# Attention in plain float32 with two heads side by side in the array, issued as one group per unit, and a router that works in quarters of the array

## The chip, the cores and the metric

The kernel runs on one core of a Trainium2 chip. The metric is the device time of one execution in microseconds (us), with the kernel's inputs and its output in device memory. TensorE (PE) does the matmuls, VectorE (DVE), ScalarE (ACT) and GpSimd (POOL) the elementwise work, and SyncE (SP) issues most of the transfers.

## The reference

Attention over a window of 128 keys with a linear bias for each head, then a dense layer with a gate, then a mixture of eight experts of which each token uses one:

```python
q, k, v: (4, 8, 576, 64) float32
scores = q @ k.T / 8 + slope[head] * -(i - j)        # kept where 0 <= i - j < 128
attn   = softmax(scores)
x      = (attn @ v) as (2304, 512)
h      = x @ w_in                                    # (512, 2048)
x      = (h * clip(h + 3, 0, 6) / 6) @ w_out         # (2048, 512)
logits = (x / |x|) @ (expert_emb / |expert_emb|).T / tau
e      = argmax(logits);  gate = softmax(logits)[e]
out    = gate * (relu(x @ w1[e]) @ w2[e])
```

## The kernel before

The 2304 tokens are cut into nine chunks of 256. A **unit** is one chunk and one pair of heads, so each chunk has four. Units of chunks 0 and 1 (class `Early`) run at the start, while the dense layer's weights arrive. The other 28 (class `Unit`) run in pieces between the dense layer's matmuls of the chunk before: `gemm1` (L780, 24 matmuls of 256 columns) and `gemm2` (L823, 12 matmuls of 512 columns), eight of each in a chunk. After a chunk's `gemm2`, `Route` turns the rows of the result (L851), works out the eight logits of a token (L869) and ranks the tokens by expert (L897, L898). From about 600 us on only the experts' matmuls are left.

The dense layer and the experts use float32 split in two float32r parts, high and low, with three matmuls for a product. A `Unit` does the same: `split_qk` splits keys and scaled queries (L579 to L592) and copies the query parts across the partitions with two DMAs of ACT's queue, `split_v` splits the values, `split_p` the flipped probabilities. So a head's scores (L625) are two matmuls of 128 rows for each block of queries, and its values (L742) two for each window of keys. `Early` does it in plain float32: its scores (L420) use 64 rows of the array for a head, its values (L474) 64 columns, with the two heads next to each other. Flips (L461, L697) are transposes of the probabilities on PE.

A batch has 576 tokens, which is two and a quarter chunks. Chunks 3, 5 and 8 lie evenly on blocks of 128 rows. Chunks 2 and 6 have blocks of 64 rows of queries and of keys, chunk 7 has one block of 64 keys, and chunk 4 has blocks of 128 but a batch's start inside. 

PE's order is that of the program: a table `todo` maps a step (a number, some 3 us) to functions, and the steps are written out by hand (`UNITS_2`, `UNIT`, `PARTS`, `FIRST`, `ROUTE`). On DVE, ACT and POOL the program's scheduler sets the order in this part. Before, a unit has two pieces of scores, two of flips and two of values, one of each for a head, spread over the steps. `I_NORM`, `I_VHI`, `I_VLO`, `I_XLO`, `I_XL3` and `I_GL` are tables that choose the engine of some steps by chunk.

Of the kernel before, what the change touches and what calls it, by code (L numbers as in the profile page):

```python
# [46 lines left out]
SECOND_1 = 2.95  # L47

FIRST = (16.97, 1.91, 2.95)

UNITS_2 = (0.3, 2.8, 5.3, 7.8)
UNIT = (11.36, 3.6)


PARTS = (
    (2.28, 5.87, 8.0, 0.86, 1.01, 5.33, 5.0, 1.94),
    (3.01, 6.0, 8.3, 0.91, 1.0, 4.93, 4.79, 1.0),
)

ROUTE = ((3.76, 4.57, 6, 8.04), (1, 1.43, 2.92, 4.5))  # L60

I_NORM = (1, 1, 0, 1, 0, 0, 0, 0, 0)
I_VHI = (0, 1, 1, 0, 0, 0, 1, 1, 0)
I_VLO = (1, 1, 0, 0, 0, 0, 0, 0, 0)
I_XLO = (0, 1, 1, 0, 1, 1, 0, 0, 1)
I_XL3 = (1, 1, 1, 1, 1, 1, 1, 1, 1)
I_GL = (1, 0, 0, 0, 1, 0, 0, 0, 1)
# [18 lines left out]
def words(t):  # L86
    return t.bitcast(F32)
# [7 lines left out]
def tile_kernel(  # L95
# [41 lines left out]
    raw = right.enter_context(tc.tile_pool(name="raw", bufs=1, side="right"))  # L137
    at1 = right.enter_context(tc.tile_pool(name="at1", bufs=1, side="right"))
# [22 lines left out]

    def either(flag):
        return V if flag else nc.gpsimd
# [43 lines left out]
    enT = const.tile([128, KD, NE], F32, name="enT")  # L207
# [7 lines left out]
    nc.gpsimd.memset(half, 0.5)  # L215
    for p in range(NP):
        for h in range(2):
            nc.gpsimd.memset(units_of[64 * h:64 * h + 64, p:p + 1], unit_of(2 * p + h))
# [28 lines left out]
    def embed():  # L247
# [12 lines left out]
        V.tensor_copy(out=enT, in_=ps[:, :, 0:NE])  # L260
# [234 lines left out]
    class Unit:  # L495
# [55 lines left out]
        def load_v(self):  # L551
            t = raw.tile([128, len(self.ks), 128], F32, tag="vr", name="vr")
# [7 lines left out]
        def transpose_qk(self):  # L560
            def turn(src, width, nm):
                t = at1.tile([128, width], F32, tag=nm, name=nm)
                V.transpose(out=t, in_=src.rearrange("p t i -> p (t i)")[:, 0:width])
                return t
# [4 lines left out]
        def split_qk(self):  # L569


            nk = self.koff[-1]
            kT, qT = self.kT, self.qT
            self.k1 = k1 = at1.tile([128, 2, 384], F32R, tag="k1", name="k1")
            self.q1 = q1 = at1.tile([128, 2, CH], F32R, tag="q1", name="q1")
            self.q2 = q2 = at1.tile([128, 2, CH], F32R, tag="q2", name="q2")
            for h in range(2):
                r, o = slice(64 * h, 64 * h + 64), slice(64 - 64 * h, 128 - 64 * h)
                nc.scalar.copy(k1[r, h, 0:nk], kT[r, 0:nk])  # L579
                V.tensor_tensor(  # L580
                    out=k1[o, h, 0:nk], in0=kT[r, 0:nk], in1=words(k1[r, h, 0:nk]), op=ALU.subtract
                )
            for h in range(2):
                r, o = slice(64 * h, 64 * h + 64), slice(64 - 64 * h, 128 - 64 * h)
                sc = unit_of(self.h0 + h)
                nc.scalar.activation(out=q1[r, h, :], in_=qT[r, 0:CH], func=AF.Copy, scale=sc)
                V.scalar_tensor_tensor(
                    out=q1[o, h, :], in0=qT[r, 0:CH], scalar=sc, in1=words(q1[r, h, :]),
                    op0=ALU.mult, op1=ALU.subtract,
                )  # L590
# [3 lines left out]
        def split_v(self):  # L594

            self.v2 = v2 = at1.tile([128, 4, 2, 128], F32R, tag="v2", name="v2")
            spans = [(r, r + x[2]) for r, x in zip(self.row, self.ks)]
            for r0, r1 in sorted(set(spans)):
# [920 lines left out]
```

## Time and profile before

| what | value |
|---|---|
| time, median of 3 runs | 852.37 us (845.07 to 852.41) |
| the profiled execution | 850.65 us, of which its span is 848.9 us |
| mean granted clock of TensorE in the span | 0.968 of full speed |
| busy share of PE, DVE, ACT, POOL | 95%, 65%, 54%, 37% |

A row of a group of instructions gives line, engine, operation, tiles, shape and count. The timeline's first two columns are a start and a duration in us. Matmuls are pipelined, so a duration covers more than the array's own time for it. The distance from the start of one piece to the start of the next says what a piece costs in a dense stretch.

### The profile page before, as it was taken

To read this page: it belongs to the slowest core of one execution; us is meant where nothing else is said; L and a number is where in the kernel's file an instruction comes from. 1 tells how busy PE (TensorE), PEld (TensorE's weight loads), DVE (VectorE), ACT (ScalarE), POOL (GpSimd) and SP (SyncE) were. 2 spreads that over 40 slices of the span, in tenths; PEclk is the share of its full clock that TensorE was granted. 3 is DMA by queue.
4 is the path that set the end of the run, shared out by engine and by line. 5 is a ranking of instruction groups with operands and counts; after the bars stand their busy time and mean duration, and the time that the engine had idled before them with its cause. 6 is when DMAs were issued, how large, how long until landed. Compare 5 with 4: busy or idle time off the path is not lost. (4 is left out here: it accounts for less than half of the span.)

```text
span 848.9 us, 16092 instructions
## 1 busy us (share of the span) xinstructions
PE 809.2 (95%) x5404; PEld 721.3 (85%) x5404; DVE 551.0 (65%) x1482; ACT 459.2 (54%) x1140; POOL 314.5 (37%) x617
## 2 busy tenths in 40 slices
PE   5899989899999999999999999999999999999994
PEld 3666578679989999988899999998899999999993
DVE  4999967575767776867677776324565566447620
ACT  6676657466646566567467565333655445435410
POOL 1000014473544556776557645123233122132300
PEclk8699999899999999999999999999999999999997
DMA  9927133323333233233233221005647655465200
GB/s 263 332 81 221 79 69 67 44 58 80 58 56 83 47 65 81 52 58 72 43 58 86 50 48 29 2 25 165 221 133 239 226 182 197 169 217 177 100 24 26
DMA packets 156664, 90.86 MB, mean 107 GB/s; under 512 B 117491, under 2 KB 134003, under 8 KB 156576
## 3 DMA queue, kind: packets, MB, share of 16 engines
q1 hardware_dynamic: 148352, 72.85, 31.4%
q10 hardware_dynamic: 4480, 7.34, 4.0%
q0 software_dynamic: 3744, 9.58, 3.3%
q8 instruction: 45, 0.74, 0.4%
q14 instruction: 43, 0.35, 0.2%
HBM read 72.76 MB, written 9.74 MB: 97 GB/s over the span
## 5 line engine op out<-in xcount | busy, mean ns | idle before, releaser
L780 PE MATMUL h_ps<-xs,w_i 128*128 128x256 f32 x1536 | 202.3, 289 | 2.0 <-ACT xs L159 2.0
L780 PEld LDWEIGHTS h_ps<-xs,w_i 128*128 128x128 f32 x1536 | 192.1, 194 | 4.5 <-ACT xs L159 2.2
L823 PE MATMUL y_ps<-w_o,gh 128*128 128x512 f32 x512 | 167.0, 408 | 1.0 <-ACT gh L159 1.0
L823 PEld LDWEIGHTS y_ps<-w_o,gh 128*128 128x128 f32 x512 | 93.9, 193 | 18.8 <-ACT gh L159 1.3
L160 DVE TENSOR_TENSOR w_e<-st,w_e 128x1024 fp32r<-128x1024 f32 x64 | 77.4, 1233 | 47.8 <-ACT w_e L159 47.8
L1060 PE MATMUL ps_u<-x,w_e 128*128 128x280 f32 (+5 forms) x768 | 104.8, 293 | 0.0
L823 PE MATMUL y_ps<-w_o,gl 128*128 128x512 f32 x256 | 102.3, 400 | 1.4 <-POOL gl L160 1.4
L1060 PEld LDWEIGHTS ps_u<-x,w_e 128*128 128x128 f32 x768 | 100.0, 188 | 0.2
L797 DVE SCALAR_TENSOR_TENSOR u<-u,h_ps 128x512 f32<-128x512 f32 x72 | 49.2, 683 | 55.0 <-ACT u L790 54.7
L790 ACT ACTIVATE u<-h_ps,three 128x512 f32<-128x512 f32 x72 | 49.3, 684 | 65.4 <-PE h_ps L780 52.0
L659 ACT ACTIVATE pt<-pt,nm 128x128 f32<-128x128 f32 (+1 forms) x128 | 49.9, 391 | 61.9 <-DVE pt L648 24.8
L1084 PE MATMUL ps_o<-hs,w_e 128*128 128x280 f32 (+4 forms) x576 | 78.4, 295 | 0.0
L1084 PEld LDWEIGHTS ps_o<-hs,w_e 128*128 128x128 f32 x576 | 76.5, 188 | 0.0
L159 ACT CAST w_e<-st 128x1024 fp32r<-128x1024 f32 x64 | 65.3, 1049 | 15.4 <-DMA st<-in_moe_w_dram 6.0
L1159 POOL DMA_INDIRECT out_dram<-ob,ids x23 | 30.4, 1321 | 108.7 <-DVE ob L1158 99.4
L611 POOL TENSOR_TENSOR v<-vr,v 128x384 fp32r<-128x384 f32 (+4 forms) x48 | 35.6, 751 | 82.0 <-ACT v L608 79.8
L823 PEld LDWEIGHTS y_ps<-w_o,gl 128*128 128x128 f32 x256 | 49.1, 192 | 14.0 <-POOL gl L160 2.3
L159 ACT CAST gh<-u 128x512 fp32r<-128x512 f32 x64 | 39.6, 619 | 29.4 <-DVE u L797 28.8
L690 POOL TENSOR_TENSOR pt<-pt,rs 128x128 f32<-128x128 f32 (+2 forms) x80 | 33.6, 440 | 45.2 <-DVE rs L677 29.8
L1068 ACT ACTIVATE hs<-ps_u 128x280 fp32r<-128x280 f32 (+5 forms) x64 | 25.7, 404 | 45.3 <-PE ps_u L1060 44.0
L639 DVE CUSTOM_DVE_ANT_0 pt<-sc_ps,table 128x256 f32<-128x256 f32 (+3 forms) x128 | 44.1, 370 | 6.6 <-PE ps_pt L697 2.6
L1018 POOL DMA_INDIRECT xg<-ybuf,ids x20 | 22.9, 1145 | 55.8 <-DMA ids<-slots 41.9
(187 smaller groups left out, 1507.2 us busy)
## 6 DMA issues: line engine op xcount, KB each, us to landing
st<-in_moe_w_dram SPq DMA_DIRECT2D x32, 512.0 KB, 4.6
st<-in_moe_w_dram SPq DMA_DIRECT2D x16, 1024.0 KB, 8.9
wst<-in_moe_w_in_dram SPq DMA_DIRECT2D x8, 1024.0 KB, 8.6
wst<-in_moe_w_out_dram SPq DMA_DIRECT2D x8, 1024.0 KB, 8.6
q<-q ACTq DMA_DIRECT2D x56, 128.0 KB, 2.2
vr<-in_v_dram SPq DMA_DIRECT2D x72, 64.0 KB, 2.2
ybuf<-ys SPq DMA_DIRECT2D x18, 256.0 KB, 2.3
kr<-in_k_dram SPq DMA_DIRECT2D x48, 48.0 KB, 2.1
```

Source lines behind the costliest of these rows:

```text
L159: nc.scalar.copy(hi, src)
L160: eng.tensor_tensor(out=lo, in0=src, in1=words(hi), op=ALU.subtract)
L611: either(I_VLO[self.c]).tensor_tensor(out=d[:, :, 1::2, :], in0=s, in1=words(d[:, :, 0::2, :]), op=ALU.subtract)
L639: V.tensor_tensor_reduce(out=pt[0:n, s0:s1], in0=self.sc_ps[0:n, s0:s1], in1=table[0:n, t0:t0 + c1 - c0], scale=-slope, scalar=3.0e38, op0 ...
L659: nc.scalar.activation(out=pt[0:n, a:a + m], in_=pt[0:n, a:a + m], func=AF.Exp, scale=-1.0, bias=nm[0:n, j:j + 1], accum_out=sm[0:n, j:j + 1],
L690: nc.gpsimd.tensor_tensor(out=w, in0=w, in1=rs[0:n, j:j + 1].to_broadcast([n, m]), op=ALU.mult)
L780: nc.tensor.matmul(hp[:, f, :], lhsT=w[:, a, kk, f * 128:(f + 1) * 128], rhs=xs[:, b, kk, :], start=(n == 0), stop=(n == 3 * KD - 1),)
L790: nc.scalar.activation(out=u, in_=hp, func=AF.Relu, bias=three, scale=1.0)
L797: V.scalar_tensor_tensor(out=u, in0=u, scalar=6.0, in1=h_t[c, i], op0=ALU.min, op1=ALU.mult)
L823: nc.tensor.matmul(y_t[c][t], lhsT=g[a][:, f, t * 128:(t + 1) * 128], rhs=w[:, b, f, :], start=(i == 0 and f == 0 and n == 0), stop=(i == ...
L1060: nc.tensor.matmul(ps, lhsT=w[:, a, kk, (f % 2) * 128:(f % 2) * 128 + 128], rhs=x[:, b, kk, c0:c1], start=(n == 0), stop=(n == 3 * KD - 1),)
L1084: nc.tensor.matmul(ps, lhsT=ws_t[j, 4 + f // 2][:, a, f % 2, d * 128:(d + 1) * 128], rhs=hs[:, b, f, 0:width(j)], start=(n == 0), stop=(n ...
```

## The change

`Unit` is written like `Early`. The splits of queries, keys, probabilities and values, with their tiles and the two DMAs of the queries, go. Scores and values are plain float32 matmuls, with the two heads of a pair in two halves of the array. Normalising moves from ACT or POOL to DVE, the low parts of `x` and of the gated hidden values go to DVE throughout, and the tables that chose engines go. A unit's scores, flips and values no longer have steps of their own for each head: at each step of `group`, PE does the values of one unit, the flips of the next and the scores of the one after it, in a row. The loads get more buffers (`raw` two, `vr` three).

The logits are turned round. The embedding (32 columns, 8 of them used) is the stationary operand, four blocks of 128 model dimensions go into four quarters of the array's columns, ACT copies the result, and a second pair of matmuls (`total`) with a table of ones (`fold`) adds up the four quarters, one step of `TOTAL` later.

```diff
-PARTS = (
-    (2.28, 5.87, 8.0, 0.86, 1.01, 5.33, 5.0, 1.94),
...
+GROUPS = (1.9, 2.8, 15.7)
+PARTS = (1.2, 1.2, 6.0, 2.78)
+TOTAL = 0.95
...
-            nc.scalar.dma_start(out=words(q2)[0:64], in_=words(q1)[64:128])
-            nc.scalar.dma_start(out=words(q2)[64:128], in_=words(q1)[0:64])
...
+        def scale(self):
+            nc.scalar.activation(out=self.qT, in_=self.qT, func=AF.Copy, scale=units_of[:, self.p:self.p + 1])
...
-        def scores(self, h):
-            sc_ps = bank([128, 512], "sc_ps")
-            r = slice(64 * h, 64 * h + 64)
+        def scores(self):
+            self.sc = [bank([128, 512], "sc_ps") for h in range(2)]
             for j, n, c0, cm, c1, s0, s1 in self.blocks():
-                for a, qq in enumerate((self.q1, self.q2)):
+                for h in range(2):
+                    r = slice(64 * h, 64 * h + 64)
                     nc.tensor.matmul(
-                        sc_ps[0:n, s0:s1], lhsT=qq[:, h, self.qoff[j]:self.qoff[j] + n], rhs=self.k1[:, h, c0:c1],
-                        start=(a == 0), stop=(a == 1),
-                    )
+                        self.sc[h][0:n, s0:s1], lhsT=self.qT[r, self.qoff[j]:self.qoff[j] + n], rhs=self.kT[r, c0:c1],
+                        start=True, stop=True,
+                    )
...
-        def values(self, h):
+        def values(self):
             acc = bank([128, CH], "acc")
...
+                for h in range(2):
                     nc.tensor.matmul(
...
+                        acc[64 * h:64 * h + 64, o:o + m], lhsT=self.vr[k0:k0 + kn, kj, 64 * h:64 * h + 64],
+                        rhs=self.pp[h][k0:k0 + kn, at:at + m],
...
+            keep_x(self.c, self.p, acc, V)
...
-        split(gh, gl, g_t[c, i], either(not I_GL[c]))
+        split(gh, gl, g_t[c, i])
...
         def logits(self):
-            self.lg = lg = bank([128, 2, NE], "lg")
+
+            ps = bank([128, CH], "lgT")
             for t in range(2):
                 for kk in range(KD):
                     nc.tensor.matmul(
-                        lg[:, t, :], lhsT=self.yT[t][:, kk, :], rhs=enT[:, kk, :], start=(kk == 0), stop=(kk == KD - 1)
-                    )
+                        ps[32 * kk:32 * kk + 32, t * 128:(t + 1) * 128], lhsT=enT[:, kk, :], rhs=self.yT[t][:, kk, :],
+                        start=True, stop=True, skip_group_check=True,
+                    )
+            self.lgT = small("lgT", (128, CH), bufs=1)
+            nc.scalar.copy(self.lgT, ps)
+
+        def total(self):
+            self.lg = lg = bank([128, 2, NE], "lg")
+            for t in range(2):
+                nc.tensor.matmul(lg[:, t, :], lhsT=self.lgT[:, t * 128:(t + 1) * 128], rhs=fold, start=True, stop=True)
...
+    def group(n):
+        n -= n_early
+        return GROUPS[0] + GROUPS[1] * n if n < 5 else GROUPS[2] + 2 * FIRST[1] * (n - 5)
...
+        t0, t1, t2 = (group(n + x) for x in range(3))
+        turn, norm, early, vearly = PARTS
...
+        at(t0 - turn, u.scale)
+        at(t0, u.scores)
         for h in range(2):
-            d = b + h * other
...
+            at(t0, u.soften, h)
...
+        at(t1, u.flip_p)
+        for h in range(2):
+            at(t1, u.unload_p, h)
+        at(t2, u.values)
```

The first place is PE in the dense layer of chunk 4, where units of chunk 5 are done. Before, a head's flips (`ps_pt`) and another's scores (`sc_ps`, four matmuls with the two query parts in turn) stand between a `gemm2` and a `gemm1` (`h_ps`), and the values (`acc`, high and low probabilities `ph` and `pl` in turn) after it:

```order
L823 MATMUL y_ps<-w_o,gl 128x512
L697 MATMUL ps_pt<-ident,pt 128x128 x2
L625 MATMUL sc_ps<-k_3912,q_3913 128x256
L625 MATMUL sc_ps<-k_3912,q_3914 128x256
L780 MATMUL h_ps<-xs,w_i 128x256 x24
L742 MATMUL acc<-ph,v_3905 128x128
L742 MATMUL acc<-pl,v_3905 64x128
```

After the change, for a unit of the same kind:

```order
L702 MATMUL h_ps<-xs,w_i 128x256 x24
L676 MATMUL acc<-ph,vr 64x128 x2
L676 MATMUL acc<-ph,vr 64x256 x2
L636 MATMUL ps_pt<-ident,pt 128x128 x4
L574 MATMUL sc_ps<-kT,qT 128x256 x4
L745 MATMUL y_ps<-w_o,gh 128x512 x2
```

Values, flips and scores of three units now stand together, and `gemm2` follows them. Two pairs of `gemm2` and `gemm1` lie between two such groups.

The second place is PE at the logits of a chunk (`lg`), with its neighbours. Before:

```order
L823 MATMUL y_ps<-w_o,gl 128x512
L869 MATMUL lg<-enT,yT 128x8 x8
L625 MATMUL sc_ps<-k_4127,q_4128 128x256
L625 MATMUL sc_ps<-k_4127,q_4129 128x256
L780 MATMUL h_ps<-xs,w_i 128x256 x24
```

After:

```order
L745 MATMUL y_ps<-w_o,gl 128x512
L792 MATMUL lgT<-yT,enT 32x128 x8
L702 MATMUL h_ps<-xs,w_i 128x256 x24
L802 MATMUL lg<-fold,lgT 128x8 x2
L745 MATMUL y_ps<-w_o,gh 128x512 x2
```

The eight narrow matmuls have become eight of 128 columns in the quarters, and two narrow ones that stand a `gemm1` later. For the last chunk the two pieces stand next to each other.

The third place is ACT at the start of the dense layer of chunk 1, around the squares of the embedding (`junk`), on which PE's transposes of the embedding depend. Before:

```order
L842 ACTIVATE ys<-y_ps 128x512
L579 CAST k_1018<-kT 64x384
L586 ACTIVATE q_1019<-qT 64x256 x2
L252 ACTIVATE junk,n_1037<-en 8x512
L591 DMA q_1020<-q_1019 64x512
```

After:

```order
L562 ACTIVATE qT<-qT,fixed 128x256
L764 ACTIVATE ys<-y_ps 128x512
L244 ACTIVATE junk,n_1020<-en 8x512
L712 ACTIVATE u<-h_ps,three 128x512
L149 CAST gh<-u 128x512
```

The splits of keys and queries have left the place ahead of the squares.

## Rows read from the trace of the kernel before

**Rows 1.** The page's first part: an engine's busy us, its share of the span and its instructions.

```profile
PE 809.2 (95%) x5404; PEld 721.3 (85%) x5404; DVE 551.0 (65%) x1482; ACT 459.2 (54%) x1140; POOL 314.5 (37%) x617
```

**Rows 2.** The waits of PE: what waited for what, us in total, times, the longest.

```profile
PE sc_ps L625 <- DMA q<-q: 4.1, 1, 4.1
PE h_ps L780 <- ACT xs L159: 2.0, 1, 2.0
...
PE ps_en L259 <- DVE en L256: 1.9, 1, 1.9
PE y_ps L823 <- POOL gl L160: 1.4, 2, 0.9
PE acc L742 <- POOL pl L711: 1.3, 1, 1.3
...
PE acc L742 <- POOL pl L715: 0.6, 1, 0.6
```

**Rows 3.** Busy time in chosen stretches: the stretch, its length, busy us and instructions of PE, PE's weight loads, DVE, ACT, POOL; then the granted TensorE clock, the DMA share and GB/s.

```profile
158.50:166.00 7.50, 7.50 (x32) 5.90 (x31) 0.60 (x2) 0.98 (x3) 0.79 (x4) 0.66 0.22 37
187.00:192.00 5.00, 5.00 (x18) 4.00 (x18) 2.65 (x10) 3.10 (x10) 1.90 (x2) 0.66 0.38 83
252.00:259.00 7.00, 7.00 (x39) 6.45 (x38) 4.32 (x14) 4.65 (x13) 1.99 (x6) 0.76 0.18 29
374.50:379.00 4.50, 4.50 (x14) 3.31 (x14) 3.42 (x10) 3.94 (x13) 2.08 (x5) 0.62 0.39 72
404.00:410.00 6.00, 6.00 (x39) 5.83 (x39) 3.81 (x24) 1.70 (x8) 1.85 (x6) 0.72 0.46 84
410.00:585.00 175.00, 175.00 (x1199) 159.49 (x1199) 104.28 (x334) 88.44 (x238) 85.34 (x176) 1.00 0.19 40
585.00:600.00 15.00, 12.51 (x78) 10.60 (x78) 7.85 (x8) 8.57 (x10) 5.08 (x4) 1.00 1.06 361
```

**Rows 4.** The timeline of ACT at the start of the dense layer of chunk 1: start, us, engine, line, operation, tiles, shape, count.

```profile
109.53 0.51 ACT L579 CAST k<-kT 64x384 fp32r<-64x384 f32 x1
110.46 0.60 ACT L842 ACTIVATE ys<-y_ps 128x512 f32<-128x512 f32 x1 [0.42 <-PE y_ps L814]
111.08 0.51 ACT L579 CAST k<-kT 64x384 fp32r<-64x384 f32 x1
111.62 0.86 ACT L586 ACTIVATE q<-qT 64x256 fp32r<-64x256 f32 x2
112.50 0.63 ACT L252 ACTIVATE junk<-en 8x512 f32<-8x512 f32 x1
```

**Rows 5.** The timeline of PE in an even chunk's units.

```profile
323.01 0.38 PE L697 MATMUL ps_pt<-ident,pt 128*128 128x128 f32 x2
323.15 0.72 PE L625 MATMUL sc_ps<-k,q 128*128 128x256 f32 x4
323.70 3.03 PE L780 MATMUL h_ps<-xs,w_i 128*128 128x256 f32 x24
326.57 0.22 PE L742 MATMUL acc<-ph,v 128*128 128x128 f32 x1
...
327.10 0.62 PE L851 MATMUL ps_y<-ident,ys 128*128 128x128 f32 x4
```

**Rows 6.** The timeline of PE in the units of class `Early` (chunk 1). A plain float32 matmul counts as two instructions here.

```profile
63.81 1.09 PE L474 MATMUL acc<-ph,stage 128*64 128x128 f32 x12
64.83 1.13 PE L420 MATMUL sc_ps<-kt,qt 64*128 64x256 f32 x8
65.90 0.66 PE L400 MATMUL ps_qk<-ident,stage 128*128 128x128 f32 x4
...
71.52 1.14 PE L420 MATMUL sc_ps<-kt,qt 64*128 64x256 f32 x8
72.59 0.66 PE L461 MATMUL ps_pt<-ident,pt 128*128 128x128 f32 x4
73.08 3.62 PE L770 MATMUL h_ps<-xf,w 128*128 128x256 f32 x16
```

**Rows 7.** The timeline of PE in units with blocks of 64 rows: first of chunk 2 (values, scores and flips of a head, and the `gemm2` after them), then of chunk 6 (flips and scores of a head, and what follows).

```profile
143.90 0.28 PE L742 MATMUL acc<-ph,v 128*128 128x64 f32 x1
...
144.88 0.77 PE L625 MATMUL sc_ps<-k,q 128*64 128x192 f32 x6
145.58 0.73 PE L697 MATMUL ps_pt<-ident,pt 64*128 64x64 f32 x3
146.24 0.72 PE L823 MATMUL y_ps<-w_o,gh 128*128 128x512 f32 x2
...
394.70 0.53 PE L697 MATMUL ps_pt<-ident,pt 128*128 128x128 f32 x3
395.16 0.77 PE L625 MATMUL sc_ps<-k,q 128*128 128x256 f32 x6
395.76 0.66 PE L851 MATMUL ps_y<-ident,ys 128*128 128x128 f32 x4
```

**Rows 8.** The timeline of PE at the logits of a chunk, and the piece after them.

```profile
337.87 1.84 PE L869 MATMUL lg<-enT,yT 128*128 128x8 f32 x16
339.57 0.71 PE L625 MATMUL sc_ps<-k,q 128*128 128x256 f32 x4
```

More of the change, by code (lines that the diff above doesn't have):

```diff
@@ L215, in tile_kernel @@
     nc.gpsimd.memset(half, 0.5)
+    nc.gpsimd.memset(enT, 0.0)
+    V.tensor_reduce(
+        out=fold, in_=ident.rearrange("p (g e) -> p e g", g=KD)[:, 0:NE, :], axis=AX.X, op=ALU.add
+    )
     for p in range(NP):
@@ L662, in soften @@
                 )
-            self.pt[h], self.sm[h] = pt, sm
+            self.pt[h] = pt
         def joint(self, i):
@@ L677, in normalise @@
             V.reciprocal(out=rs[:, 0:nq], in_=rs[:, 0:nq])
-            if self.even and not I_NORM[self.c]:
-                w = pt.rearrange("p (j l k) -> p j l k", j=2, l=2)[:, :, 0, :]
-                nc.gpsimd.tensor_tensor(
-                    out=w, in0=w, in1=rs[:, 0:2, None].to_broadcast([128, 2, 128]), op=ALU.mult
-                )
-                return
             for j, n, *_ in self.blocks():
@@ new lines, in normalise, with flip_p @@
+                V.tensor_scalar(out=w, in0=w, scalar1=rs[0:n, j:j + 1], scalar2=None, op0=ALU.mult)
+        def flip_p(self):
+            self.ps_pt = bank([128, 2, CH], "ps_pt")
+            for h in range(2):
+                pt = self.pt[h]
+                for i, n, *_ in self.blocks():
+                    a, m = self.joint(i)
+                    nc.tensor.transpose(
+                        out=self.ps_pt[0:m, h, self.qoff[i]:self.qoff[i] + n], in_=pt[0:n, a:a + m],
+                        identity=ident[0:n, 0:n]
+                    )
@@ new lines, in unload_p, with part @@
+        def unload_p(self, h):
+            self.pp[h] = pp = at2.tile([128, 512], F32, tag=("ph", "pl")[h], name="ph")
+            def part(o, p, src, n, r0, r1):
+                nc.scalar.copy(o, src)
+                dims = [list(x) for x in ([[0, n]] if n > 1 else [])]
+                if r1 > r0:
+                    nc.gpsimd.affine_select(
+                        out=p[r0:r1], in_=o[r0:r1], compare_op=ALU.is_gt, fill=0.0, base=r0,
+                        pattern=dims + [[-1, o.shape[-1]]], channel_multiplier=1,
+                    )
+                    nc.gpsimd.affine_select(
+                        out=o, in_=o, compare_op=ALU.is_ge, fill=0.0, base=0,
+                        pattern=dims + [[1, o.shape[-1]]], channel_multiplier=-1,
+                    )
+            ps = self.ps_pt[:, h, :]
+            if self.even:
+                assert self.own[1] - self.own[0] == self.prev[1] - self.prev[0] == 256
@@ L726, in split_p @@
                 assert self.own[0] == 128 and self.prev[0] == 0
-                part(o, p, self.ps_pt.rearrange("p (j k) -> p j k", j=2), 2, 0, 128)
+                p, o = (pp.rearrange("p (j l k) -> p j l k", j=2, l=2)[:, :, l, :] for l in range(2))
+                part(o, p, ps.rearrange("p (j k) -> p j k", j=2), 2, 0, 128)
                 return
@@ L1319, in tile_kernel @@
         at(g + d[2], r.logits)
-        at(g + d[2], r.choose)
+        at(g + d[2] + TOTAL, r.total)
+        at(g + d[2] + TOTAL, r.choose)
         at(g + d[3], r.ranks)
@@ L1358, in tile_kernel @@
     after(LAST[2], r.logits)
+    after(LAST[3], r.total)
     after(LAST[3], r.choose)
```

164 lines of the change are left out of this document (28 added, 136 removed).

## Prediction

> **What bounds the kernel now.** I read the busy shares first, then PE's waits, then the granted clock by stretches, and last the timeline of PE in the dense layer, where all of the changed work lies. PE is busy 95% of the span, DVE 65%, ACT 54% and POOL 37% [rows 1]. From 410 to 585 us PE is busy for all of 175 us at a granted clock of 1.00 [rows 3]. So time goes up or down with what PE has to do there, and with what makes it wait. Work that leaves DVE, ACT and POOL is worth nothing by itself. It counts where one of their results came too late for PE.
>
> There are such places. PE waits 4.1 us for the copied query parts, 2.0 us for the split `x` of a new chunk, 1.3 and 0.6 us for POOL's work on the low probabilities, 1.9 us for the embedding, and 1.4 us for a low part that POOL makes [rows 2]. Behind such waits PE stays busy at a lower clock: granted shares of 0.66, 0.66, 0.76 and 0.62 over 7.5, 5, 7 and 4.5 us [rows 3]. A share between 0.5 and 1 is a mixture of the two levels, 1.2 and 2.4 GHz. One more stretch, 404 to 410 us, has 0.72 although PE was busy all the time. What stood there was logits and the values of a unit with 64-row blocks, small matmuls in a row.
>
> The sum below is against the profiled execution, 850.65 us (span 848.9). The median of the runs shown is 852.37, that is 1.7 us above.
>
> **Waits and clock, minus 18.7.** The two DMAs of the queries go, and with them the 4.1 us. The low probabilities go, so POOL has half of the selects to do and no value splits or normalising (1.3 and 0.6 us). The values come out with both heads in place, so one copy and one subtraction lead to `x` where there were a copy and an addition for each head ahead of them (2.0 us), and the flips, the scores and a `gemm2` cover these. Together 8.0 us [rows 2]. What the slow stretches lose is length times the missing share: 7.5 x 0.34 + 5 x 0.34 + 7 x 0.24 + 4.5 x 0.38 + 6 x 0.28 = 9.3 us [rows 3]. The embedding's squares start on ACT at 112.50. Without the splits ahead of them they could start when the copy of 110.46 ends, at 111.06 [rows 4]. That is 1.4 of the 1.9 us. If PE's new order brings the same waits back elsewhere, all of this is lost; I take it as gained because the work behind each wait is removed and not moved.
>
> **Units with even blocks, plus 1.7.** Before, flips and scores of a head cost 323.01 to 323.70 = 0.69 us, the values 326.57 to 327.10 = 0.53 us and about 0.06 us at the next piece's start, so a unit 2 x 1.28 = 2.56 us [rows 5]. After it, the nearest rows are those of `Early`, the same matmuls at the granted clock of a warm PE: scores 71.52 to 72.59 = 1.07, four flips 72.59 to 73.08 = 0.49, values 63.81 to 64.83 = 1.02 us, and 0.1 us at the border [rows 6]. That is 2.7 us, 0.14 more. So plain float32 is no gain on PE by itself: one of its matmuls of 256 columns takes 3.62 / 8 = 0.45 us [rows 6], a float32r one 2.87 / 24 = 0.12 [rows 5], nearly a quarter. Half as many matmuls and two heads at once only give that back. Twelve units: +1.7. If the groups lose the borders between pieces it may be 0; ends -5 and +4.
>
> **Units with 64-row blocks.** In chunk 2 a head's values cost 143.90 to 144.88 = 0.98, scores 0.70, three flips 0.66 us [rows 7], a unit 4.7. Three flips cost nearly five times what two even ones cost in front of their successor (0.14, rows 5): the change of row height is dear, some 0.17 us for each. After it, I take the scores at 1.25 (the even ones have as many columns, 512; four more instructions), the flips at 1.2 (the same six, one border less) and the values at 1.1 (384 columns of 512, so 0.77, and 0.3 for the change to 64 rows). That is 3.6, a gain of 1.1 for each of four units: -4.4. In chunk 6 flips and scores of a head cost 394.70 to 395.76 = 1.06 [rows 7]; with values as in chunk 2 that is 4.1, and 3.4 after: -2.8. For chunks 4 and 7 I take a value between the even units and these, -0.25 for each of eight: -2.0. Together -9.2; the ends are 0 (every 64-row piece as dear as before) and -15 (only columns count).
>
> **Logits, minus 4.9.** Before they cost 337.87 to 339.57 = 1.70 us, 16 instructions of 106 ns [rows 8], nine times. After it the eight matmuls have 128 columns. If the quarters run together they need a quarter of their columns' time: the values of `Early`, two halves together, took 1.02 us for 512 columns a half [rows 6], so 256 columns a quarter are some 0.5 us, and with twice the instructions per column 0.63. `total` has four narrow instructions, 0.43 us. So 1.06 instead of 1.70, eight times: -5.1. In the last chunk `total` directly follows, and PE waits for ACT's copy; +0.2. Ends: -7 with nothing but columns, +3 if the quarters run one after another.
>
> **The low part on DVE, minus 0.7.** In chunk 8 PE waited 1.4 us for POOL's low part of the hidden values [rows 2]. DVE makes it now, but it also splits the experts' weights there, at a DMA share of 1.06 [rows 3]: half.
>
> **New falls of the clock, plus 6.** A group in chunks 2 and 6 is 3.3 to 3.6 us of small matmuls in a row, longer than the light stretch ahead of 404 us. Seven groups have six flips with 64-row blocks. A fall costs about 1.7 us by the five stretches above. I take half of them: 6; ends 0 and 14.
>
> The sum is 850.65 - 18.7 + 1.7 - 9.2 - 4.9 - 0.7 + 6 = 824.85, so **825 us**. What covers the rest: between a unit's scores and its flips lie two `gemm1` of 2.87 us [rows 5] and two `gemm2` with as many columns, some 11.5 us for the chain of softmax, in which DVE and ACT have less to do than before. New waits in ACT's queue: `total` depends on a copy behind the exponentials, with one `gemm1` as cover. Queued behind DVE's normalising, which waits for ACT's exponentials, are the gate and the low part of the hidden values, on which `gemm2` waits; a `gemm2` and a `gemm1` lie between.
>
> **The rivals.** *The array empties at the changes of tile shape, or the clock falls in most groups.* The first is a rule: the Trainium skill, TensorEngine Tiling (Array Packing), Key Properties, says that a change of tiling mode, not just of tile, drains TensorE. The trace agrees for row heights (the 64-row flips above) and hardly for column widths alone, since the values of before change between 128 and 64 columns at each of their six matmuls and take 0.53 us [rows 5]. As a mechanism of this kernel: if each change costs the 0.17 us of the flips, four more changes in each of 28 groups than the rows of `Early` hold are +19 us at most; half of it is nearer, since these rows begin and end at such changes. With that, or with the clock falling behind 14 groups, the time is 835 to 843. Against it: `Early` has flips, values and scores in a row at normal prices [rows 6].
>
> *The work gets shorter but the waits come back*, because a group needs four banks of PSUM at once, or for another reason: 825 + 13 = 838. For it: eight banks in all, two of them held by the dense layer. Against it: the hidden values' banks are free within about a `gemm1`.
>
> *The two heads don't run together* in the new shapes, so the change doesn't do what it says. Scores and values then cost some 0.85 us more each, 1.7 in a unit: 825 + 28 x 1.55 = 868. Against it: four matmuls of 256 columns one after another would be 4 x 0.45 = 1.8 us, and the rows show 1.07 and 1.02 [rows 6].
>
> *Slower by waiting in the groups.* PE's order is fixed, and one late result (flips for a normalised row, values for POOL's select) holds up values, flips, scores and the next `gemm2` together. With a wait of 1 us and a fall of the clock of 1.7 us behind it, a group loses 2.7 us. From 825 the change breaks even at ten such groups; with all 28 it would be about 900, with fifteen 866. For it: POOL pieces were late before [rows 2]. Against it: POOL loses more than half of its work there.
>
> **How the numbers follow.** The forecast has 0.60 (815 to 834), tile shapes or clock 0.16, the waits that come back 0.09, better than 815 (no falls, and 64-row pieces by their columns) 0.06, heads one after another 0.04, waiting groups 0.05. The range of 808 to 845 holds the first four but for their tails and leaves out the two slow ones. About 1% is what a measurement of this kernel can tell from no change. Below 843.8 lie the first four almost entirely: faster 0.87; within 1% 0.06, from the tails; slower 0.07.
>
> **What would show it.** In the changed profile: no wait for a query DMA, and the low-clock stretches behind waits gone; a unit's group in an even chunk at 2.5 to 2.7 us from the values' start to the next dense matmul, in chunk 2 at 3.3 to 3.9; the eight logit matmuls at 0.6 to 0.9 us and `total` at 0.4; DVE's and POOL's busy time lower with no effect of its own; the experts' part as long as before. The prediction is wrong if PE shows waits at groups, if the granted clock falls behind them, or if scores and values take over 1.5 us each.

## The result, and the profile after

The changed kernel takes 825.3 us (median of 4 runs, 824.7 to 826.0), the kernel before, beside it on the same chip, 849.1 us (median of 4, 845.1 to 852.4). The ratio is 0.972, with an interval from 0.967 to 0.978. The profiled execution of the changed kernel took 824.70 us, with a span of 822.9 us and a mean granted clock of 0.983, against 850.65, 848.9 and 0.968.

The page's first part, to be read beside [rows 1]:

```profile
PE 789.3 (96%) x5440; PEld 679.6 (83%) x5440; DVE 469.9 (57%) x1364; ACT 390.7 (47%) x961; POOL 145.6 (18%) x273
```

POOL lost more than half of its work, DVE and ACT 81 and 69 us, and PE 20. The waits of PE after the change (beside [rows 2]; the lines left out belong to the start of the kernel and to the experts):

```profile
PE y_ps L745 <- ACT gh L149: 3.9, 1, 3.9
...
PE lg L802 <- ACT lgT L797: 0.5, 1, 0.5
PE ps_n L872 <- DVE seen L842: 0.4, 1, 0.4
...
PE y_ps L745 <- DVE gl L150: 0.3, 1, 0.3
```

The query parts, the split `x`, the low probabilities and the embedding are in it no more. Busy time in stretches of the dense layer, with the columns of [rows 3]:

```profile
110.00:120.00 10.00, 9.87 (x74) 8.50 (x73) 6.47 (x31) 5.86 (x19) 0.58 (x1) 1.00 0.32 83
120.00:556.00 436.00, 435.64 (x3131) 372.32 (x3130) 229.40 (x909) 197.19 (x600) 80.39 (x185) 1.00 0.21 40
556.00:563.00 7.00, 6.28 (x40) 5.27 (x38) 2.46 (x3) 2.72 (x4) 2.25 (x3) 1.00 0.97 323
563.00:570.00 7.00, 3.60 (x9) 2.38 (x10) 5.00 (x7) 4.10 (x7) 0.00 (x0) 0.76 1.06 371
570.00:585.00 15.00, 15.00 (x109) 13.33 (x111) 8.55 (x11) 10.08 (x19) 0.60 (x1) 1.00 0.43 137
```

From 120 to 556 us PE is without a gap to speak of, at a granted clock of 1.00. None of the 28 groups brought a wait or a fall of the clock, nor do they in the traces of the three variants below with the same groups (old logits, earlier weights, both). One bad place is left, 562 to 570 us, in the dense layer of the last chunk.

The timeline of PE at a chunk's logits, at its `total` with a group of chunk 2 behind it, at a group of chunk 6, and at one of an even chunk (beside [rows 5, 7, 8]):

```profile
132.92 0.65 PE L792 MATMUL lgT<-yT,enT 128*32 128x128 f32 x16
133.50 0.73 PE L745 MATMUL y_ps<-w_o,gh 128*128 128x512 f32 x2
...
136.35 0.51 PE L802 MATMUL lg<-fold,lgT 128*128 128x8 f32 x4
136.79 1.04 PE L676 MATMUL acc<-ph,vr 128*64 128x64 f32 x16
137.76 1.26 PE L636 MATMUL ps_pt<-ident,pt 64*128 64x64 f32 x6
138.95 1.44 PE L574 MATMUL sc_ps<-kT,qT 64*64 64x192 f32 x12
140.32 3.14 PE L702 MATMUL h_ps<-xs,w_i 128*128 128x256 f32 x24
...
356.36 1.14 PE L676 MATMUL acc<-ph,vr 128*64 128x128 f32 x16
...
359.54 0.73 PE L745 MATMUL y_ps<-w_o,gh 128*128 128x512 f32 x2
...
490.36 1.09 PE L676 MATMUL acc<-ph,vr 128*64 128x128 f32 x12
491.38 0.66 PE L636 MATMUL ps_pt<-ident,pt 128*128 128x128 f32 x4
491.96 1.13 PE L574 MATMUL sc_ps<-kT,qT 64*128 64x256 f32 x8
493.03 0.50 PE L745 MATMUL y_ps<-w_o,gh 128*128 128x512 f32 x1
```

From start to start the logits are 133.50 - 132.92 = 0.58 us and `total` 0.44. The group of chunk 2 is 140.32 - 136.79 = 3.53 us, that of chunk 6 3.18, the even one 2.67.

The bad place, PE first and then ACT:

```profile
553.39 3.04 PE L702 MATMUL h_ps<-xs,w_i 128*128 128x256 f32 x24
...
559.25 3.03 PE L702 MATMUL h_ps<-xs,w_i 128*128 128x256 f32 x24
566.14 1.08 PE L745 MATMUL y_ps<-w_o,gh 128*128 128x512 f32 x2 [3.85 <-ACT gh L149]
567.48 0.80 PE L745 MATMUL y_ps<-w_o,gl 128*128 128x512 f32 x1 [0.26 <-DVE gl L150]
```

```profile
558.73 1.05 ACT L149 CAST w_e<-st 128x1024 fp32r<-128x1024 f32 x1 [2.68 <-DMA st<-in_moe_w_dram]
561.38 1.05 ACT L149 CAST w_e<-st 128x1024 fp32r<-128x1024 f32 x1 [1.60 <-DMA st<-in_moe_w_dram]
562.33 0.68 ACT L712 ACTIVATE u<-h_ps,three 128x512 f32<-128x512 f32 x1
564.52 1.04 ACT L149 CAST w_e<-st 128x1024 fp32r<-128x1024 f32 x1 [1.51 <-DMA st<-in_moe_w_dram]
565.47 0.61 ACT L149 CAST gh<-u 128x512 fp32r<-128x512 f32 x1
```

ACT has a cast of expert weights (`w_e`) in its queue ahead of the high part `gh` of the hidden values. The cast waits for its transfer until 564.52, `gh` starts at 565.47, and PE's `gemm2` waits for `gh` until 566.14. The delay began further ahead: `u`, from which `gh` is made, comes from the `gemm1` that PE began at 553.39 and left at about 556.3, but two more such casts, waiting until 558.73 and 561.38, stand ahead of it in ACT's queue, and it starts at 562.33. Behind PE's wait the clock is low: 0.76 over the 7 us above.

Where the 26 us went in these two profiled executions can be added up from the starts of PE's pieces. From the first `gemm1` of chunk 1 to the last `gemm2` it was 494.2 us before and is 467.6 us now, 26.6 less; the start of the kernel gives nothing, and the experts' part is 0.7 us longer. All pieces of the timeline in that stretch, each from its start to the next piece's, are:

| pieces | before, us | after, us |
|---|---|---|
| flips, scores and values | 90.6 | 78.4 |
| logits and `total` | 13.7 | 7.6 |
| `gemm1` and `gemm2`, with the waits and the slow clock in them | 382.3 | 372.1 |
| transposes, ranks and the rest | 7.6 | 9.4 |

### The profile page after: what moved, and what is told of

Its sections match the earlier page's. It is cut to its first block, busy times and chain, and to the rows that moved or that the text cites. A ratio compares the mean times of both kernels' runs of the same rounds, so it can differ in the third digit from the quotient of the medians.

```text
span 822.9 us, 15070 instructions
## 1 busy us (share of the span) xinstructions
PE 789.3 (96%) x5440; PEld 679.6 (83%) x5440; DVE 469.9 (57%) x1364; ACT 390.7 (47%) x961; POOL 145.6 (18%) x273
## 5 line engine op out<-in xcount | busy, mean ns | idle before, releaser
L702 PE MATMUL h_ps<-xs,w_i 128*128 128x256 f32 x1536 | 195.7, 284 | 0.0
L745 PE MATMUL y_ps<-w_o,gh 128*128 128x512 f32 x512 | 164.7, 403 | 3.9 <-ACT gh L149 3.9
L745 PEld LDWEIGHTS y_ps<-w_o,gh 128*128 128x128 f32 x512 | 92.1, 190 | 26.9 <-ACT gh L149 6.0
L150 DVE TENSOR_TENSOR gl<-u,gh 128x512 fp32r<-128x512 f32 x64 | 45.8, 715 | 35.6 <-ACT gh L149 34.8
L649 POOL TENSOR_SCALAR_AFFINE_SELECT ph<-ph 128x256 f32<-128x256 f32 (+3 forms) x80 | 32.1, 410 | 167.3 <-ACT ph L646 162.0
L587 DVE CUSTOM_DVE_ANT_0 pt<-sc_ps,table 128x256 f32<-128x256 f32 (+3 forms) x128 | 42.1, 368 | 4.2 <-PE sc_ps L574 4.0
L1000 DVE SCALAR_TENSOR_TENSOR hs<-ps_u,hs 128x280 fp32r<-128x280 f32 (+5 forms) x64 | 27.9, 443 | 20.3 <-ACT hs L999 20.3
```

The lines of the kernel that those rows point to most:

```text
L150: eng.tensor_tensor(out=lo, in0=src, in1=words(hi), op=ALU.subtract)
L587: V.tensor_tensor_reduce(out=pt[0:n, s0:s1], in0=self.sc[h][0:n, s0:s1], in1=table[0:n, t0:t0 + c1 - c0], scale=-slope, scalar=3.0e38, op0 ...
L649: nc.gpsimd.affine_select(out=p[r0:r1], in_=o[r0:r1], compare_op=ALU.is_gt, fill=0.0, base=r0, pattern=dims + [[-1, o.shape[-1]]], channel ...
L702: nc.tensor.matmul(hp[:, f, :], lhsT=w[:, a, kk, f * 128:(f + 1) * 128], rhs=xs[:, b, kk, :], start=(n == 0), stop=(n == 3 * KD - 1),)
L745: nc.tensor.matmul(y_t[c][t], lhsT=g[a][:, f, t * 128:(t + 1) * 128], rhs=w[:, b, f, :], start=(i == 0 and f == 0 and n == 0), stop=(i == ...
```

## The experiments

**Each half of the change alone.** First the kernel before with the new logits and nothing else (the tiles moved a little to make room):

```diff
-ROUTE = ((3.76, 4.57, 6, 8.04), (1, 1.43, 2.92, 4.5))
+ROUTE = ((3.76, 4.57, 6, 8.46), (1, 1.43, 2.92, 4.5))
+TOTAL = 0.95
...
-                        lg[:, t, :], lhsT=self.yT[t][:, kk, :], rhs=enT[:, kk, :], start=(kk == 0), stop=(kk == KD - 1)
+                        ps[32 * kk:32 * kk + 32, t * 128:(t + 1) * 128], lhsT=enT[:, kk, :], rhs=self.yT[t][:, kk, :],
...
-        at(g + d[2], r.choose)
+        at(g + d[2] + TOTAL, r.total)
+        at(g + d[2] + TOTAL, r.choose)
```

> The kernel before with the new router alone: logits in quarters, and their total one step later; attention as it was. By the traces a chunk's logits cost 1.70 us before and 0.58 + 0.37 us after the change, eight chunks in the dense layer: 6 us less than before, and the fall of the clock at 404 us (1.7 us) may go too. If the router's gain is only there because the attention around it is short, the difference is under 2 us.

Measured: 848.7 us (10 runs) beside 847.7 for before, ratio 1.001 (0.9985 to 1.004). The pieces are as short as in the changed kernel, but PE's waits in the trace of this kernel say where the gain stayed:

```profile
PE rk L912 <- DVE oh L903: 3.2, 3, 1.2
PE y_ps L829 <- POOL gl L161: 3.1, 2, 2.0
PE acc L748 <- POOL ph L717: 2.7, 2, 1.4
```

The fall of the clock at 404 to 410 us is gone in this trace, but four others stand in its dense layer, three of them behind waits for POOL and one behind the ranks. The ranks `rk` wait for the choice `oh`, which now comes later from a DVE that still has the split attention to do. So I set the additions and the ranks later in the same kernel:

```diff
-ROUTE = ((3.76, 4.57, 6, 8.46), (1, 1.43, 2.92, 4.5))
+ROUTE = ((3.76, 4.57, 6, 9.6), (1, 1.43, 2.92, 4.5))
...
-        at(g + d[2] + TOTAL, r.total)
-        at(g + d[2] + TOTAL, r.choose)
+        late = TOTAL * (1 if c == NCH - 2 else 2)
+        at(g + d[2] + late, r.total)
+        at(g + d[2] + late, r.choose)
```

> The kernel before with the new logits alone, as in the earlier run of the router alone, but the additions of the four quarters stand twice as far behind the logits, and the ranks 1.1 steps later. It tests why the router alone gained nothing although its logits cost 0.57 + 0.36 us instead of 1.70. Theory (TensorE waited for the choice: 3.2 and 1.0 us for the ranks' operands and 1.3 us for the copy of the logits, and ran slowly behind it): with later ranks these waits go, and the time falls by 4 to 6 us from 848.7, to 843 to 845. Rival (the waits of this kernel move about whatever is changed, since ScalarE, VectorE and GpSimd are late with the split attention): other waits take their place, and the time stays at 847 to 850.

Measured: 845.7 us (8 runs) beside 849.9, ratio 0.998 (0.995 to 1.002). The interval holds no change, so this is inconclusive as a time. In its trace the ranks wait 1.1 us instead of 3.2, and others have come up: 1.8 us for the split `x`, 1.4 for `gh`, 1.2 for a normalised row. From the first `gemm1` of chunk 1 to the last `gemm2`, PE waits 15.6 us in the trace of the router alone and 13.6 in this one, against 12.4 in that of before, although the wait for the query parts (4.1) is in neither. That is what the rival said: in the kernel before, a shorter piece of PE is at least in part paid back as waiting for ACT, DVE and POOL. How much of it is not shown, since single executions differ by as much (see the slow clock, below).

The other half is the changed kernel with the old logits:

```diff
-                        ps[32 * kk:32 * kk + 32, t * 128:(t + 1) * 128], lhsT=enT[:, kk, :], rhs=self.yT[t][:, kk, :],
+                        lg[:, t, :], lhsT=self.yT[t][:, kk, :], rhs=enT[:, kk, :], start=(kk == 0), stop=(kk == KD - 1)
...
-        at(g + d[2] + TOTAL, r.total)
-        at(g + d[2] + TOTAL, r.choose)
+        at(g + d[2], r.choose)
```

> The changed kernel with the logits of before (sixteen narrow instructions) and the choice in its old place. My theory: 6 us more than the changed kernel, some 831 us, with no fall of the clock in the dense layer, since the groups by themselves showed none. The rival, that long stretches of small matmuls pull the clock down: logits of 1.70 us beside groups of 2.7 to 3.5 us bring falls of some 1.7 us each, and the time is 836 us or more.

Measured: 828.1 us (4 runs), ratio 0.978 (0.975 to 0.981), only 2.8 us above the changed kernel's 825.3, which did not run beside it. In the traces the stretch of the dense layer differs by 3.3 us. So the attention carries nearly all of the gain. The rival is refuted: the clock stays at 1.00 in the dense layer up to the last chunk's wait. The logits cost 1.70 us again, but the wait for `gh` in the last chunk is 2.8 us here and 3.9 in the changed kernel. PE comes to that place 5.7 us later than in the changed kernel, and `gh` only 4.7.

**The stall in the last chunk.** The changed kernel with the first expert's weights ahead of the row numbers in SP's queue:

```diff
-PLACE_0 = (6.5, 9.0, 7.64, 2.08, 1.1, 1.0)
+PLACE_0 = (6.5, 9.0, 6.65, 2.08, 2.2, 1.0)
...
-    at(g + PLACE_0[0], load_ids, 0, range(n_first))
+    at(g + PLACE_0[0] + 0.5, load_ids, 0, range(n_first))
```

> The changed kernel with one edit at the end of the dense layer: the first two loads of the first expert's weights are issued ahead of the three loads of the row numbers, and the weight loads, the casts behind them and the row numbers are set about 1 us earlier or later in the table so that SyncE's queue and ScalarE's come out in that order. It tests what the new stall of chunk 8 is worth: TensorE waited 3.9 us for the high part gh, queued on ScalarE behind a cast of weights that waited for its transfer, and then ran about 6 us at a granted clock of 0.76. Theory (the queue order makes the stall): the weights land some 4 us earlier, the casts are done before gh is due, the wait goes and the clock stays at 1.00 there, so the time falls from 825 by 4 to 6 us, to 819 to 821. Rival (the transfers as a whole bound this stretch, 350 GB/s and a DMA share above 1): the wait moves to a later weight tile or to the gathered rows, and the time stays at 824 to 826.

Measured: 821.1 us (4 runs, 820.4 to 824.6), 4.2 less than the changed kernel's 825.3. The two did not run side by side, and beside the kernel before this one has the ratio 0.972 (0.963 to 0.981), as the changed kernel had. So the 4 us rest on the times as they stand and on the trace. Stretches around the former stall, and ACT there:

```profile
553.00:560.00 7.00, 7.00 (x50) 6.51 (x49) 3.15 (x6) 3.53 (x4) 2.02 (x2) 1.00 1.08 350
560.00:567.00 7.00, 6.32 (x39) 5.22 (x39) 4.76 (x6) 4.26 (x6) 1.97 (x2) 1.00 1.05 374
```

```profile
556.53 1.05 ACT L149 CAST w_e<-st 128x1024 fp32r<-128x1024 f32 x1 [0.44 <-DMA st<-in_moe_w_dram]
557.49 0.68 ACT L712 ACTIVATE u<-h_ps,three 128x512 f32<-128x512 f32 x1
559.16 1.05 ACT L149 CAST w_e<-st 128x1024 fp32r<-128x1024 f32 x1 [0.99 <-DMA st<-in_moe_w_dram]
560.11 0.61 ACT L149 CAST gh<-u 128x512 fp32r<-128x512 f32 x1
```

The cast ahead of `gh` starts at 559.16 instead of 564.52, PE waits 0.2 us for `gh` and 1.0 us for `gl`, and the clock stays at 1.00. The stretch of the dense layer is 463.6 us instead of 467.6. The transfers run at the same rate as before, 350 to 374 GB/s; it was the order of the queues. (The edit sets the weights earlier and the row numbers later at once; the two were not tried apart.) Of the whole profiled execution, 4.1 us shorter, 1.3 lie ahead of the dense layer, and the experts' part gives 1.2 back. The same edit in the kernel with the old logits shows what the logits are worth when no stall lies behind them (its edit is the two above together):

> The changed kernel with the old logits (as in the run of the attention alone) and with the earlier weights of the first expert. Beside the kernel with the earlier weights it gives the worth of the new logits where no stall at the end of the dense layer can hide it. Theory (the new logits save 0.7 us of TensorE in each of eight chunks, and the stall took half of it back): if the stall is gone in both, this one is 5 to 6 us slower than the other, so 825 to 826. Rival (the new logits save less, since their copy and their later choice cost something elsewhere): the two are 2 to 3 us apart, as were the kernels without this edit (828.1 and 825.3).

Measured: 824.9 us (4 runs, 824.1 to 827.9), 3.9 above its partner by the medians, and 5.0 by the spans of the profiled executions (823.8 and 818.8). By the medians that lies between the two expectations, by the spans at the lower end of the theory, whose 5 to 6 was somewhat too much. And the same edit in the kernel before:

> The kernel before with the earlier weights of the first expert alone, the edit that took 4 us from the changed kernel. Its own stall at that place was 2.5 us of waiting, without a fall of the granted clock behind it. Theory (the stall is made by the order of the queues, in both kernels): 2 to 3 us less than before, 845 to 846. Rival (in the kernel before GpSimd's low parts are the late ones, which the edit doesn't touch): 847 to 849.

Measured: 850.1 us (median of 10 runs; one execution of 2121 us among them, at a mean granted clock of 0.373, is unexplained) beside 849.9, ratio 1.000 (0.998 to 1.002). PE waits 1.3 us for POOL's low parts there, nearly as before (1.4), and 0.5 instead of 1.0 us for `gh`, so 1.9 us in all instead of 2.5, too little for this measurement. So the rival holds: in the kernel before there was next to nothing to be had at this place, and the 4 us are a debt of the new kernel. The time alone would not show that, since a wait in the experts' part of this trace is longer, 3.2 us where before had 0.7:

```profile
PE ps_x L1030 <- DMA xg<-ybuf,ids: 3.2, 1, 3.2
```

Whether the edit brings it is open: the router alone with later ranks, without this edit, shows 3.1 us of the same wait.

**The copied query parts.** The kernel before without its two DMAs, both products of a head with the same query part:

```diff
-            self.q2 = q2 = at1.tile([128, 2, CH], F32R, tag="q2", name="q2")
+            self.q2 = q1
...
-            nc.scalar.dma_start(out=words(q2)[0:64], in_=words(q1)[64:128])
-            nc.scalar.dma_start(out=words(q2)[64:128], in_=words(q1)[0:64])
```

> The kernel before without the two DMAs that copy the query parts across the partitions; both matmuls of the scores use the first tile, so the low parts of the queries meet the wrong keys and the output is not the reference's. My theory: PE's wait of 4.1 us for that DMA and the 2.6 us of slow clock behind it go: 6 to 7 us less than an execution of before that has the wait. The times of before fall into two, 845 and 852 us. If that wait is what sets them apart, all times of this kernel lie near 845, and none near 852. The rival: something else is late at that place (the selects of POOL, the split of the keys), and the time stays.

Measured: 837.2 us (4 runs, 833.9 to 842.0), ratio 0.989 (0.984 to 0.994), 10 us less by the medians. The interval, 5 to 14 us, holds the 6 to 7 that were expected. Its scores are not the reference's, but the experts' part is as long as before (241.4 us, 242.0 before). In its trace not only the wait of 4.1 us has gone, but also some others, and the dense layer has two stretches at the low clock instead of six. The wait for the split `x` in its trace is

```profile
PE h_ps L778 <- ACT xs L159: 0.7, 1, 0.7
```

instead of 2.0 us [rows 2]. That the query wait explains why two executions of before differ by 7 us is not borne out: without it four executions still differ by 8.

**Do two heads run together?** The changed kernel with the loop over heads outermost, so that one head's matmuls all come before the other's, the same instructions:

```diff
-            for j, n, c0, cm, c1, s0, s1 in self.blocks():
-                for h in range(2):
+            for h in range(2):
+                for j, n, c0, cm, c1, s0, s1 in self.blocks():
...
-            for x, (kj, kn, at, m, users) in enumerate(self.wins):
-                o, k0 = self.qoff[users[0]], self.row[kj]
-                for h in range(2):
+            for h in range(2):
+                for x, (kj, kn, at, m, users) in enumerate(self.wins):
+                    o, k0 = self.qoff[users[0]], self.row[kj]
```

> The changed kernel with the loops of scores and values exchanged: all matmuls of one head, then all of the other, so that neighbours in the queue use the same half of the array. The same instructions and the same output. My theory, that the two heads run together because they alternate: scores and values of an even unit cost 1.7 to 1.9 us instead of 1.06 and 1.02, a unit some 1.6 us more, 28 units 40 to 45 us, some 867 us. The rival, that the price of these matmuls does not come from running together: within 5 us of the changed kernel.

Measured: 853.1 us (8 runs), ratio 1.007 (1.0025 to 1.011), some 28 us above the changed kernel. The loss lies unevenly. The timeline of PE at a group of this kernel, with the values of chunk 7 and the scores of an even chunk:

```profile
485.50 2.38 PE L676 MATMUL acc<-ph,vr 128*64 128x256 f32 x12
487.81 0.66 PE L636 MATMUL ps_pt<-ident,pt 128*128 128x128 f32 x4
488.39 1.14 PE L574 MATMUL sc_ps<-kT,qT 64*128 64x256 f32 x8
489.46 0.74 PE L745 MATMUL y_ps<-w_o,gh 128*128 128x512 f32 x2
```

The scores take 1.07 us as with the heads in alternation, although the second head's matmuls stand four instructions behind the first's. The values take 2.31 us instead of 1.17. What differs is that the scores of an even chunk have one shape throughout, and the values of chunk 7 have not. Pieces of chunks 2 and 6, whose shapes change too, double in the same way (values 1.91 and 2.12 us instead of 0.97 and 1.07), even values, with as many instructions as those of chunk 7 but one tile shape, rise from 1.02 to 1.29. That the shape decides is read from these pieces; no run changes the shape alone. All scores, flips and values of the dense layer rise from 78.4 to 103.7 us. So the expectation of 40 to 45 us was wrong in size since part of the overlap stays.

The expectation also left out the clock. In this trace it falls behind a group of 4.6 us, 353.19 to 357.79, while PE is busy throughout:

```profile
351.50:357.50 6.00, 6.00 (x43) 4.45 (x42) 2.62 (x10) 2.44 (x9) 1.49 (x7) 1.00 0.16 34
357.50:361.50 4.00, 4.00 (x13) 3.16 (x12) 3.91 (x24) 2.93 (x13) 0.59 (x2) 0.57 0.14 26
```

Four longer groups of this kernel, of 5.3 and 5.4 us, have no fall behind them.

The control is the changed kernel with both heads' scores in the same half:

```diff
-                    r = slice(64 * h, 64 * h + 64)
+                    r = slice(0, 64)
```

> The changed kernel with the scores of both heads in the same 64 rows of the array: the second head reads the first head's queries and keys, so its scores are not its own and the output is not the reference's; instructions and columns are as before. It is the control for the claim that two heads run beside each other in two halves. Theory (two halves are two streams; one half is one): an even unit's scores go from 1.07 us to 1.8 to 1.95 us, and 28 units make 21 to 26 us, so 846 to 852. Rival (the price is the instructions', not the array's): 1.07 us as before and 825.

Measured: an even group's scores go from 1.07 to 331.90 - 329.98 = 1.92 us,

```profile
329.98 1.99 PE L574 MATMUL sc_ps<-kT,qT 64*128 64x256 f32 x8
331.90 0.73 PE L745 MATMUL y_ps<-w_o,gh 128*128 128x512 f32 x2
```

and all scores of the dense layer from 30.6 to 53.5 us. That is the theory: 23 us from the halves in the scores alone. The whole time, 1109.8 us, is not to be compared, since other scores send the tokens to other experts, and a loop for tokens beyond an expert's capacity follows, in whose lines PE waits 117 us. The dense layer's stretch is 496.0 us, 28.4 more, of which 5.5 are not the scores'. The granted clock around a group of chunk 2 (138.27 to 143.29) shows part of them:

```profile
131.00:141.50 10.50, 10.50 (x87) 8.25 (x86) 7.81 (x42) 5.82 (x24) 1.38 (x7) 1.00 0.30 55
141.50:149.00 7.50, 7.50 (x34) 6.61 (x34) 3.84 (x24) 2.57 (x13) 1.06 (x6) 0.54 0.19 31
```

PE is busy all the time here and the clock falls nevertheless, at about 142 us, inside the group, to little above the lower of its levels, 1.2 GHz. A second fall, from 159.0 us on, follows the next group (4.4 us).

**Is the row of pieces itself good or bad?** The changed kernel with the flips 0.95 steps and the scores 1.6 steps later, so that a dense piece stands between each two:

```diff
+APART = (0.95, 1.6)
...
-        at(t0, u.scores)
+        at(t0 + APART[1], u.scores)
...
-        at(t1, u.flip_p)
+        at(t1 + APART[0], u.flip_p)
```

> The changed kernel with the same instructions, but values, flips and scores of a group stand apart: values where they were, flips one step of the table later and scores another half step later, so that a dense piece lies between each two. It tests what standing in one row is worth, and whether a group of small matmuls is a risk for the clock. Theory (a piece costs its columns and a border of some 0.1 us, and nothing else): two more borders in each of 28 units, so 3 to 6 us more, 828 to 831, with the same flips, scores and values apart from the borders, and a granted clock of 1.00. Rival (each change between dense matmuls and pieces of other tile shapes empties the array): 10 us more and above. Second rival (nothing, the border is hidden): 824 to 827.

Measured: 830.9 us (4 runs, 830.1 to 833.6), 5.5 above the changed kernel. The number is within the theory, but not for its reason alone. Flips standing alone are mostly cheaper (0.35 instead of 0.58 us in an even unit, 0.53 in front of logits), a dense piece beside a small one dearer. And this kernel has waits in its groups, since less lies between flips and values:

```profile
PE acc L677 <- POOL ph L650: 1.0, 1, 1.0
PE ps_pt L637 <- DVE pt L629: 0.6, 1, 0.6
PE acc L677 <- POOL ph L654: 0.5, 1, 0.5
```

Behind the two at 150 us the clock is 0.76 over 7 us, 1.7 us more. In this profiled execution these waits and their clock are 3.8 of the 8.4 us by which its dense layer is longer than the changed kernel's. The stall in the last chunk is there in both, but here the low clock behind it lasts longer, 572.5 to 579.3 us instead of 566.3 to 569.7, which is some 1.1 us more (an estimate: half of PE's busy time in it). The rest, about 4 us, is what borders can have cost. An emptying of the array worth 10 us or more doesn't show.

## Why the prediction came out, step by step

The forecast was 825.0, the time is 825.3. The sum went from 850.65 to 824.85, the profiled execution to 824.70. Yet several terms were off, and cancelled.

**Waits (8.0 and 1.4): right.** All the waits named are gone: 8.0 us, the embedding's 1.9 in full instead of 1.4, and one of 0.4 (`ps_n`) is new. That is 9.5.

**Slow clock (9.3): right in kind, and too small.** All five stretches are at 1.00 now. A sixth, right behind the embedding's wait, was left out of the sum. The stretch in the trace of before:

```profile
115.00:120.00 5.00, 4.85 (x29) 4.86 (x30) 1.97 (x5) 1.02 (x3) 1.19 (x2) 0.66 0.23 40
```

With 5 x 0.34 = 1.7 it makes 11.0. Its size belongs to this execution. The kernel before with earlier weights has the order of before on every engine up to 570 us, and in its trace the same matmuls, from the first `gemm1` of chunk 1 to the one at 583.04 us before and 574.58 there, take 8.1 us less: 6.5 us of waits instead of 9.9, and three stretches at the low clock instead of six.

**Units (+1.7 and -9.2): the new prices right, the old ones too high.** Even 2.7 predicted, 2.67 measured; chunk 2 3.6 and 3.53; chunk 6 3.4 and 3.18; chunks 4 and 7 2.31 and, by their own pieces, 2.25 and 2.71. All 28 units: 12 x 2.7 + 4 x 3.6 + 4 x 3.4 + 8 x 2.31 = 78.9 predicted, 78.4 measured. On the side of before the same sum is 86.4 (with 2.56 for chunks 4 and 7), while the table has 90.6 us, of which 6.1 are the waits for query and low parts, and some 2.4 the slow clock behind them (an estimate, from these pieces against their like elsewhere), so 82.1. The step that failed is the price of 4.7 for chunk 2, from one head's row with values at 0.98 and scores at 0.70 [rows 7], where others of its values took 0.80 and of its scores 0.55 to 0.64, and of 2.56 for even units, whose scores took 0.47 in many places instead of 0.55. So the pieces gave about 3.7 us instead of 7.5. Longer dense neighbours of the many separate pieces of before give some of that back: what is left for units and borders, once everything else in this list is taken from the 26.6, is about 5.

**Logits (-4.9): right.** 0.63 and 0.43 predicted, 0.57 and 0.36 to 0.44 measured in the middle chunks; 0.49 us of waiting in the last chunk instead of 0.2. The pieces are 6.1 us shorter, their neighbours some 0.1 us dearer each, and the measured worth is 3.9 to 5.0 us where no stall covers it. In the changed kernel a stall that is 1.1 us longer stands against it, which is a part of why only 2.8 us showed there.

**New falls of the clock (+6): wrong.** None came behind a group in the changed kernel, nor in the same kernel with the weights earlier. I had reasoned from one stretch of small matmuls in before, 404 to 410 us [rows 3]. Such falls do exist: the control with both heads in one half has two, in and behind groups of 5.0 and 4.4 us, and the heads in turn have one behind a group of 4.6 us. The changed kernel's groups are shorter, 3.5 us at most. That the length is the reason is not shown.

**Low part in the last chunk (-0.7): wrong, with the other sign.** Before, 2.5 us of waiting at a clock of 1.00, now 3.9 and 0.3 of waiting and 7 x 0.24 = 1.7 of slow clock, so +3.3. I looked at DVE's low part and at the share of the DMA, and not at what stood in ACT's queue ahead of the high part. The earlier weights took some 4 us back. By accident the two mistakes, 6 too much and 4 too little, nearly cover each other, and the too high prices of before most of the rest.

**The rivals.** Heads not together: refuted by the control, since they would have cost 23 us in the scores alone. (Its price of 1.55 us a unit comes from 1.8 - 1.07 and 1.8 - 1.02, about 1.5, and not from the 0.85 and 1.7 that stand beside it.) Emptying at changes of tile shape: not at the group's borders, since the new prices are those of `Early`. But inside a pair of heads a change of shape does stop one half for the other when the heads come in turn. That fits, in kind, the rule of the Trainium skill, TensorEngine Tiling (Array Packing), Key Properties, that a change of tiling mode drains TensorE. With the heads in alternation little of it is left: the values of chunk 7 take 1.17 us, those of an even chunk 1.02. Waits that come back or stand in groups: none did in a group, with POOL at 18% of the span; with the pieces apart they begin (2.1 us).

## What to carry to other kernels

Where one engine sets the time, add up its pieces on both sides of the change from start to start over a whole stretch, and not from one row: the new prices here were right to 0.5 us in 78, the old ones 4 us too high. Look in every queue for what stands ahead of the operand that the bound engine needs next, above all a cast or copy that waits for a transfer; that cost 4 us here and setting the weight loads ahead of the row numbers got them back. When removing side work takes the waits out of the bound engine, the slow clock behind them can go too: in the profiled execution that was as much as the waits. And one profiled execution is one sample: two with the same order of work differed by 8.1 us in the dense layer by their waits and the clock behind them.

## What the runs showed of the hardware

Two halves of the array run as two streams even where one head's matmuls stand four instructions behind the other's (scores 1.07 us in either order, 1.92 in one half), as long as the tile shapes stay. With more instructions of one shape part of that is lost (even values 1.29 against 1.02 us). Values whose shapes change within a head take twice the time with the heads in turn (2.31 against 1.17 us in chunk 7).

A granted clock near its lower level came while PE was busy throughout: 0.54 over 7.5 us in and behind a group of 5.0 us (values, flips and scores in one half), 0.57 over 4 us behind one of 4.6 us with the heads in turn. Other groups of that kernel, of 5.3 and 5.4 us, among them the corresponding one at 138.5 to 143.8, have no fall. Nor is the order of the pieces enough. Before, PE went at the full clock behind the logits and flips of 134.28 to 136.72 us; the kernel before with earlier weights has the same pieces at 132.44 to 134.89, and a fall behind them. First before, then that run:

```profile
137.00:141.00 4.00, 4.00 (x22) 2.98 (x22) 3.79 (x25) 2.91 (x12) 1.53 (x4) 1.00 0.37 68
135.00:139.00 4.00, 4.00 (x11) 3.14 (x12) 3.40 (x21) 2.90 (x11) 1.37 (x3) 0.57 0.40 75
```

What tells the cases apart is open.

A flip of 128 by 128 in a row of pieces costs more in front of scores (four in 0.58 us) than in front of `gemm1` (0.35).
